# Prologue of an adaLN, linear-attention and MLP block: three query chunks folded in 64 by 64 tiles, modulation rows paired, layer-norm statistics moved

## The chip, the cores and the metric

The kernel runs on one core of one Trainium2 chip. The metric is the device time of one execution in microseconds. The core has five engines that this text names as its profile does: PE (TensorE; PEld is its weight load), DVE (VectorE), ACT (ScalarE), POOL (GpSimd) and SP (SyncE, which here only issues DMAs).

## The reference, cut to what matters

```python
mod = (silu(c) @ w_mod).reshape(1, 6, 1, 640)
sa, ca, ga, sb, cb, gb = mod[:, 0], ..., mod[:, 5]
h = layernorm(x) * (1 + ca) + sa                    # x: 2048 x 640
qkv = h @ wqkv                                      # 32 heads of 20
pq = einsum("bhsd,hdf->bhsf", q, w_phi)             # and pk from k
phi_q = concat([softmax(pq), softmax(-pq)])         # and phi_k from pk
kv = einsum("bhsf,bhsd->bhfd", phi_k, v)
z = phi_k.sum(over s)
o = (phi_q @ kv) / (phi_q . z + 1e-6)
x = x + ga * (o @ wo)
h = layernorm(x) * (1 + cb) + sb
x = x + gb * (relu(h @ w1 + b1) ** 2 @ w2 + b2)     # 640 -> 1728 -> 640
```

## The kernel before

Tokens come in 16 tiles of 128, handled in pairs `j`; the 640 features are five chunks `d` of 128. The feature map `w_phi` is multiplied into the weights of q and k once, at the start ("fold"), so that a projection gives pq and pk at once. Precision is kept by splitting each matrix into a high part in `fp32r` and a low part, the difference; each product is then three matmuls (`three`).

The change touches the prologue, up to the first attention tiles. There the order on all five engines is written out by hand: a `manual_schedule` block (`first`) keeps every engine in program order. So an instruction that waits holds up all that stands behind it on its engine.

The parts of the prologue, in their order:

- `load_raw`, `load_x`, `load_wm`: SP issues the loads: raw k weights, the first token pair `x0`, raw q weights, the modulation weights `wm` of chunks 0 to 4, then `x1` and the v weights. ACT issues two small ones (`bd`, `c`).
- DVE builds `bd_t`, block-diagonal copies of `w_phi`, from `bdc` and a mask that POOL makes.
- Warm-up matmuls (`WARM`, `SHORT`) on PE.
- `fold(nm, d)` (L276): six matmuls of 120 rows by 128 columns, with 120 (once 40) moving columns, into a pair of PSUM tiles. In f32 each matmul is two passes on PE, so a fold shows as 12 records. Its `split` copies both PSUM tiles to the high part on ACT (L283) and takes the low part on DVE (L92).
- `stats` (L556 to L561): mean and variance of a token pair on DVE, then four small POOL instructions; `scale` (L566) normalizes it on ACT. `x0`'s statistics stand behind the split of k's chunk 3.
- `mod_rows2` (L582): the modulation vector of a chunk, c-weighted sums of `wm`, as ten f32 matmuls in four column tiles of 32; `mod_sb` (L590) copies it to SBUF on ACT; `mod_cols2` transposes it on PE (L595) and sums on DVE into `cols_a` (L597).
- `t_in` (L358): PE transposes normalized `x0` into PSUM. `out0(d)` scales and shifts chunk `d` on ACT (`hf`, L369), copies the high part on ACT (`hT`, L370) and takes the low part on DVE (L92).
- `k_step(d)`: chunk `d`'s contribution to k of the first two token tiles, 12 matmuls into four PSUM tiles `pk`.
- Behind the five k steps: ACT casts v's first weight chunk (`v_hi`, L665) and copies k out of PSUM (`to_sb`, L429); DVE and ACT go on to the feature map, and PE to the query projection `do_q(0)` (`pq`).

PSUM tiles of the tag `pj` come in four buffers, two to a fold or projection, taken in turn: `pq`'s first pair is that of the first token tile's `pk`, and the fold of q3 takes the pair of q1. The fold of q0 uses two tiles of another tag, `kvp`. After the prologue PE's order stays fixed, and the other engines' order is set by a planner for a part of the way.

The heart of the prologue's order before:

```python
    for d in range(4):
        fold("k", d)()
    n0 = stats(XB[0], "a0")
    fold("k", 4)()
    fold("q", 0, kvp[1:])()
    fold("q", 1)()
    scale(XB[0], *n0)
    fold("q", 2)()
    split = fold("q", 3)
    mod_rows2(0)
```

Of the kernel before, what the change touches and what calls it, by code (L numbers as in the profile page):

```python
# [12 lines left out]
ALU = mybir.AluOpType  # L13
AX = mybir.AxisListType

P = 128
S = 2048
D = 640
H = 32
DH = 20  # L20
F = 1728
NT = S // P
NC = D // P
NF = 14
FS = [128] * 13 + [64]
GR = [(120 * g, 120) for g in range(5)] + [(600, 40)]
NG = len(GR)
NU = 11
HEAD_AT = [(h % 3 + 3 * (h // 12), h // 3 % 4, h) for h in range(H)]
HEAD_AT.sort()  # L30
HALF = D // 2
# [1 line left out]
V_HEADS = ((0, 19), (19, H - 1))  # L33
EPS = 1e-5
POSTPONED = 4
WARM = 9
SHORT = 7
KEPT = NT - POSTPONED
W2_AT = 48
PLAIN = 2  # L40
# [15 lines left out]
def kernel(  # L56
# [6 lines left out]
    wq1: bass.AP,  # L63
    wv: bass.AP,
    bd: bass.AP,
    c: bass.AP,
    w_ss: bass.AP,
    w_mod: bass.AP,
# [7 lines left out]
    nc = tc.nc  # L76
# [34 lines left out]
    def tok2(tag, name, at=0, pool=None):  # L111

        bufs = 1
        if tag == "w":
            tag = f"w{next(w_at)}"
        elif pool is None:
            bufs = BUFS.get(tag, 1)
        t = (pool or mem).tile([P, 2 * D + (W2_AT if tag == 'late' else 128 if tag in W_LONG else 0)], F32, tag=tag, name=name, bufs=bufs)
        return t[:, at : at + 2 * D].rearrange("p (s d) -> p s d", s=2)

    def row(tag, name):
        return (pc if tag in ("s3", "s4") else mem).tile([P, D], F32, tag=tag, name=name, bufs=BUFS[tag])
# [19 lines left out]
    def tp(name):  # L142
# [4 lines left out]
    kvp = [psK.tile([P, 512], F32, name=f"kvp{b}") for b in range(3)]  # L147
# [6 lines left out]
    ones = const.tile([P, P], F32, name="ones")  # L154
    nc.gpsimd.memset(ones, 1.0)

    bdc = row("s3", "bdc")
# [3 lines left out]
                            pattern=[[-DH, 6]], channel_multiplier=1)  # L161
    nc.gpsimd.affine_select(out=own, in_=own, compare_op=ALU.is_ge, fill=0.0, base=DH - 1,
                            pattern=[[DH, 6]], channel_multiplier=-1)
    ident = const.tile([P, P], F32, name="ident")
    make_identity(nc, ident)
    neg = const.tile([P, P], F32R, name="neg")
    plus = const.tile([P, 1], F32, name="plus")
    nc.gpsimd.memset(plus, 0.0)
# [9 lines left out]

    vt = [pc.tile([P, NU * 64], F32, name=f"vt{i}")[:, : H * (DH + 1)].rearrange("p (h d) -> p h d", d=DH + 1) for i in range(2)]
    rs_q = pc.tile([P, NT, 2 * H], F32, name="rs_q")  # L180
# [20 lines left out]

    nc.scalar.dma_start(bdc[:120, :120], bd)
    nc.scalar.dma_start(c_t, c)
    bd_t = row("s4", "bd_t")
    raw, WM, RV, XB = {}, {}, {}, {}

    def load_raw(nm, w5, w1, ds=range(NC)):
        if 0 in ds:
            raw[nm] = [tok2("w", f"raw_{nm}{i}") for i in range(3)]
            nc.vector.memset(raw[nm][2][:, 1], 0.0)  # L210
        for d in ds:
            nc.sync.dma_start(raw[nm][d // 2][:, d % 2], w5[d * P : (d + 1) * P])
            if d == 0:
                nc.sync.dma_start(raw[nm][2][:40, 1], w1)

    def load_x(j):
        XB[j] = tok2(f"x{j % 2}", f"xb{j}")
# [2 lines left out]
    def load_wm(d):  # L220
        WM[d] = flat(tok2(("k", "k", "q0", "q1", "w")[d], f"wm_{d}"))
        nc.sync.dma_start(WM[d], w_ss[d * P : (d + 1) * P])
# [4 lines left out]
    load_raw("k", wk5, wk1)  # L227
    load_x(0)
    load_raw("q", wq5, wq1, range(4))
    for d in range(2):  # L230
        load_wm(d)
    load_raw("q", wq5, wq1, (4,))
    for d in range(2, NC):
        load_wm(d)
    load_x(1)
    for d in range(NC):
        if d % 2 == 0:
# [28 lines left out]
    def fold(nm, d, p=None):  # L266

        w = wslot(f"w{nm}{d}")
        W[nm, d] = w
        p = p or pj(f"fold{nm}{d}")  # L270
        for g, (o, n) in enumerate(GR):
            if g < 5:
                r = raw[nm][d // 2][:120, d % 2, g * P : (g + 1) * P]
            else:
                r = raw[nm][2][:120, 1, d * P : (d + 1) * P]
            nc.tensor.matmul(  # L276
                p[g // 3][:, (g % 3) * 120 : (g % 3) * 120 + n], r, bd_t[:120, g * 120 : g * 120 + n],
                start=True, stop=True,
            )

        def split():
            for h, (a, b) in enumerate(((0, 360), (360, 640))):
                nc.scalar.activation(w[:, 0, a:b], p[h][:, : b - a], AF.Copy)  # L283
                lo(w[:, 1, a:b], p[h][:, : b - a], w[:, 0, a:b])

        return split
# [261 lines left out]
    def stats(xt, nm):  # L548

        st = small([P, 2, 2, 6], "st", f"st{nm}")  # L550
        mv = small([P, 2, 2], "mv", f"mv{nm}")
        sq = small([P, 2], "sq", f"sq{nm}")
        nb = small([P, 2], "nb", f"nb{nm}")
        for i in range(2):
            for h in range(2):
                nc.vector.bn_stats(st[:, i, h], xt[:, i, h * HALF : (h + 1) * HALF])  # L556
            nc.vector.bn_aggr(mv[:, i], st[:, i])
        nc.gpsimd.tensor_scalar(sq, mv[:, :, 1], EPS, None, op0=ALU.add)
        nc.gpsimd.tensor_tensor(sq, sq, mhalf, op=ALU.pow)
        nc.gpsimd.tensor_tensor(nb, mv[:, :, 0], sq, op=ALU.mult)  # L560
        nc.gpsimd.tensor_scalar(nb, nb, -1.0, None, op0=ALU.mult)  # L561
        return nb, sq

    def scale(xt, nb, sq):
        for i in range(2):
            nc.scalar.activation(xt[:, i], xt[:, i], AF.Identity, bias=nb[:, i : i + 1], scale=sq[:, i : i + 1])  # L566
# [6 lines left out]
    def mod_rows2(*ds):  # L573

        p = tp(f"mrow{ds[0]}")
        for m, d in enumerate(ds):
            MR[d] = p[:, m * P : m * P + P]
            for k in range(NC):
                for s in range(2):
                    c = 2 * (k % 2) + s  # L580
                    a = 256 * k + P * s
                    nc.tensor.matmul(  # L582
                        MR[d][32 * c : 32 * c + 32], cs[:, k : k + 1].to_broadcast([P, 32]), WM[d][:, a : a + P],
                        start=(k < 2 and m == 0), stop=(k >= NC - 2), skip_group_check=True,
                    )

    def mod_sb(*ds):
        for d in ds:
            t = MR[d, "sb"] = row("s1", f"msb{d}")[:, :P]
            nc.scalar.activation(t, MR[d], AF.Identity, bias=plus[:, 0:1])  # L590

    def mod_cols2(*ds):
        at = {d: half(0, 1)[:, P * (d % 2) : P * (d % 2) + P] for d in ds}
        for d in ds:
            nc.tensor.transpose(at[d], MR[d, "sb"], ident)  # L595
        for d, p in at.items():
            nc.vector.tensor_reduce(  # L597
                cols_a.rearrange("p (s d) -> p s d", s=2)[:, :, d],
                p.rearrange("p (h s r) -> p s h r", h=2, s=2)[:, :, :, 0], axis=AX.X, op=ALU.add,
            )  # L600
# [4 lines left out]
    mem.tile([P, 80], F32, tag="gap2", name="gap2", bufs=1)  # L605
    PP = [pj(f"pk{t}") for t in range(0)]

    def k_step(d):
        w = W["k", d]
        for t in range(2):  # L610
            s = slice(t * P, (t + 1) * P)
            for h, (a, b) in enumerate(CUT):
                mm(PP[t][h][:, : b - a], three(HT[0][:, d, 0, s], HT[0][:, d, 1, s], w[:, 0, a:b], w[:, 1, a:b]),
                   first=(d == 0), last=(d == NC - 1))

    def out0(d):
        t_out(cols_a, HT[0], d, "a0", TR[d])

    warm = tp("warm")
    for i in range(WARM):  # L620
        nc.tensor.matmul(warm[:, :P], ones, ones, start=True, stop=True)
    for i in range(SHORT):
        nc.tensor.matmul(warm[:1, :1], ones[:, :1], ones[:, :1], start=True, stop=True)
    for d in range(4):
        fold("k", d)()
    n0 = stats(XB[0], "a0")
    fold("k", 4)()
    fold("q", 0, kvp[1:])()
    fold("q", 1)()
    scale(XB[0], *n0)  # L630
    fold("q", 2)()
    split = fold("q", 3)
    mod_rows2(0)
    mod_sb(0)
    for d in range(NC):
        t_in(XB[0], d, TR[d])
    split()
    mod_cols2(0)
    out0(0)
    mod_rows2(1)  # L640
    mod_sb(1)
    split = fold("q", 4)
    mod_cols2(1)
    split()
    mod_rows2(2)
    mod_sb(2)
    load_x(2)
    PP += [pj(f"pk{t}") for t in range(2)]
    rows_at, cols_at = {1: (3, 4)}, {1: (2,), 2: (3, 4)}
    for d in range(NC):  # L650
        mod_cols2(*cols_at.get(d, ()))
        if d + 1 < NC:
            out0(d + 1)
        if d in rows_at:
            mod_rows2(*rows_at[d])
        k_step(d)
        mod_sb(*rows_at.get(d, ()))
        if d == 1:
            n1 = stats(XB[1], "a1")
        if d == 3:  # L660
            scale(XB[1], *n1)

    def v_hi(d):
        W["v", d] = wslot(f"wv{d}")
# [46 lines left out]
    for t in range(2, NT - 2):  # L711
        j, i = divmod(t, 2)
# [12 lines left out]
        p = proj("v", t, *([(1, 0, lambda: t1(j + 1, 4))] if t == NT - 3 else []))  # L725
# [489 lines left out]
    for j in range(NB):  # L1215
        nxt = j + 1 < NB
        b, c = 2 * j + 5, 2 * j + 6
# [63 lines left out]
        if j == 7:  # L1281
            t2(0, 4)
            p = tp("gbt")[:NC, :P]
# [347 lines left out]
    for j in range(NB):  # L1631
# [5 lines left out]
        for n in range(NP):  # L1637
            down = lambda k: prev and (down_plain if plain(*prev) else down_pair)(*prev, k)
            twice = not plain(j, n)
            m = NP * j + n - NP - 1  # L1640
# [96 lines left out]
    by_hand.__exit__(None, None, None)  # L1737


_INS = ["x", "wk5", "wk1", "wq5", "wq1", "wv", "bd", "c", "w_ss", "w_mod", "wo", "w1", "b1", "w2", "b2"]  # L1740


# [56 lines left out]
```

## Time and profile before

| | us |
|---|---|
| median of 3 runs | 748.23 |
| lowest, highest | 747.89, 750.46 |
| the profiled execution's own time | 746.04 |
| its span, first to last instruction | 744.3 |
| PE busy | 736.7 |
| DVE busy | 599.0 |
| ACT busy | 454.4 |

The granted TensorE clock was 1.00 over the whole span. In a timeline row stand the start, the length, engine, line, operation, the tiles written and read, the count, and in brackets the idle time of the engine ahead of it with what ended it. In the chain of waits stand start, length and the work that the end of the span is traced back to. Matmuls are pipelined and their ends are modelled, so a busy PE says only that something was in it; starts are firmer than ends.

### The profile page before, as it was taken

To read this page: it belongs to the slowest core of one execution; us is meant where nothing else is said; L and a number is where in the kernel's file an instruction comes from. 1 tells how busy PE (TensorE), PEld (TensorE's weight loads), DVE (VectorE), ACT (ScalarE), POOL (GpSimd) and SP (SyncE) were. 2 spreads that over 40 slices of the span, in tenths; PEclk is the share of its full clock that TensorE was granted. 3 is DMA by queue.
4 is the path that set the end of the run, shared out by engine and by line. 5 is a ranking of instruction groups with operands and counts; after the bars stand their busy time and mean duration, and the time that the engine had idled before them with its cause. 6 is when DMAs were issued, how large, how long until landed. Compare 5 with 4: busy or idle time off the path is not lost.

```text
span 744.3 us, 16676 instructions
## 1 busy us (share of the span) xinstructions
PE 736.7 (99%) x6537; PEld 718.8 (97%) x6537; DVE 599.0 (80%) x1089; ACT 454.4 (61%) x1060; POOL 168.1 (23%) x352
## 2 busy tenths in 40 slices
PE   9999999999999999999999999999999999999997
PEld 9999999999999889998999999999999999999997
DVE  6598988978999999999655777877786776777766
ACT  5767666667863365567687667475573747647431
POOL 2001101001000347647303040231321313222110
PEclk9999999999999999999999999999999999999999
DMA  9912341343432354754885567897667768667461
GB/s 325 344 37 107 120 129 56 107 142 108 139 111 72 99 168 167 166 129 107 210 249 169 151 198 260 272 312 210 185 187 200 211 183 241 185 177 215 129 183 36
DMA packets 58801, 126.47 MB, mean 170 GB/s; under 512 B 7438, under 2 KB 16403, under 8 KB 58723
## 3 DMA queue, kind: packets, MB, share of 16 engines
q1 hardware_dynamic: 38636, 79.20, 32.6%
q0 software_dynamic: 17504, 40.90, 21.8%
q10 hardware_dynamic: 2583, 5.30, 1.9%
q8 instruction: 51, 0.84, 0.5%
q14 instruction: 27, 0.22, 0.1%
HBM read 100.74 MB, written 29.89 MB: 176 GB/s over the span
## 4 chain that ended last, share of the span: by engine, by line
PE 83%; DVE 10%; ACT 3%; issue 2%; POOL 1%; DMA 1%; ACTq 0%; DVEq 0%; POOLq 0%
PE up L82 25%; PE acc L82 18%; PE pwo L82 8%; PE pk L82 7%; PE pv L82 5%; PE acc3x L82 5%; PE pq L82 5%; PE te L950 2%; DVE dn L882 1%; DVE sk L444 1%; PE foldk L276 1%; PE numa L82 1%; DVE ek L436 1%; DVE ek L446 1%; DVE scr L880 1%
## 5 line engine op out<-in xcount | busy, mean ns | idle before, releaser
L82 PE MATMUL up<-h,w 128*128 128x256 f32 x1640 | 204.6, 276 | 0.1
L82 PEld LDWEIGHTS up<-h,w 128*128 128x128 f32 x1640 | 196.4, 188 | 0.7 <-DVE h L92 0.5
L1345 ACT ACTIVATE ft<-up,b_t 128x256 f32<-128x256 f32 x104 | 48.9, 471 | 95.7 <-PE up L82 95.3
L82 PE MATMUL acc<-w,ra 128*128 128x384 f32 x452 | 97.4, 335 | 0.0
L1346 DVE TENSOR_TENSOR ft<-ft 128x256 f32<-128x256 f32 x104 | 44.3, 426 | 42.9 <-ACT ft L1345 41.5
L82 PE MATMUL pwo<-wo,ot 128*128 128x384 f32 (+1 forms) x480 | 78.5, 314 | 0.0
L82 PE MATMUL pq<-wq,hT 128*128 128x384 f32 (+1 forms) x480 | 75.6, 312 | 0.0
L82 PEld LDWEIGHTS acc<-w,ra 128*128 128x128 f32 x452 | 72.7, 188 | 0.9 <-DVE ra L92 0.6
L82 PE MATMUL pk<-wk,hT 128*128 128x384 f32 (+1 forms) x480 | 73.1, 309 | 0.1
L82 PEld LDWEIGHTS pwo<-wo,ot 128*128 128x128 f32 x480 | 69.8, 188 | 2.8 <-issue 2.7
L82 PEld LDWEIGHTS pq<-wq,hT 128*128 128x128 f32 x480 | 71.1, 188 | 0.7 <-issue 0.5
L82 PE MATMUL pv<-wv,hT 128*128 128x384 f32 (+1 forms) x480 | 71.7, 307 | 0.0
L82 PEld LDWEIGHTS pk<-wk,hT 128*128 128x128 f32 x480 | 70.4, 188 | 1.0 <-DVE hT L92 0.5
L82 PEld LDWEIGHTS pv<-wv,hT 128*128 128x128 f32 x480 | 70.1, 188 | 0.0
L92 DVE TENSOR_TENSOR ra<-ft,ra 128x384 fp32r<-128x384 f32 (+2 forms) x86 | 36.8, 449 | 32.6 <-ACT ra L1369 18.8
L1455 POOL DMA_DIRECT2D ring_a<-td_a x34 | 18.5, 543 | 117.3 <-PE acc L82 106.3
L1369 ACT ACTIVATE ra<-ft 128x384 fp32r<-128x384 f32 x48 | 25.2, 526 | 28.4 <-DVE ft L1346 22.4
L82 PE MATMUL acc3x<-w,ra 128*128 128x256 f32 x231 | 39.5, 277 | 0.0
L82 PEld LDWEIGHTS acc3x<-w,ra 128*128 128x128 f32 x231 | 37.2, 188 | 0.0
L444 DVE TENSOR_REDUCE sk<-ek 128x64 f32<-128x1280 f32 x16 | 23.7, 1482 | 14.6 <-ACT ek L439 10.1
L1360 DVE TENSOR_TENSOR ft<-ft 128x128 f32<-128x128 f32 x136 | 33.4, 287 | 1.2
L335 POOL TENSOR_SCALAR sma<-sma 128x2 f32<-128x2 f32 x6 | 2.1, 343 | 133.7 <-ACT xb L334 133.7
(258 smaller groups left out, 1448.7 us busy)
## 6 DMA issues: line engine op xcount, KB each, us to landing
ring_c<-td_c POOLq DMA_DIRECT2D x34, 384.0 KB, 3.9
ring_a<-td_a POOLq DMA_DIRECT2D x34, 384.0 KB, 3.4
ring_b<-td_b POOLq DMA_DIRECT2D x34, 256.0 KB, 3.5
esp<-eq SPq DMA_DIRECT2D x12, 640.0 KB
el<-esp SPq DMA_DIRECT2D x12, 640.0 KB
rw<-in_w SPq DMA_DIRECT2D x23, 320.0 KB
wm<-in_w_mod SPq DMA_DIRECT2D x20, 320.0 KB
xb<-in_x SPq DMA_DIRECT2D x8, 640.0 KB
```

Of the source, the lines that this page charges most:

```text
L82: nc.tensor.matmul(o, a, b, start=first and i == 0, stop=last and i == len(terms) - 1, skip_group_check=skip,)
L92: (eng or nc.vector).tensor_tensor(out_lo, full, hi.bitcast(F32), op=ALU.subtract)
L276: nc.tensor.matmul(p[g // 3][:, (g % 3) * 120 : (g % 3) * 120 + n], r, bd_t[:120, g * 120 : g * 120 + n], start=True, stop=True,)
L436: nc.vector.tensor_tensor(heads(e[:, s]), heads(t), over(mx[:, s]), op=ALU.subtract)
L444: nc.vector.tensor_reduce(s, heads(flat(e)), axis=AX.X, op=ALU.add)
L446: nc.vector.tensor_tensor(heads(flat(e)), heads(flat(e)), over(s), op=ALU.mult)
L950: nc.tensor.transpose(p[:124, a : a + P], EU[2 * j + i][:, 2 * g + c, :124], ident)
L1345: nc.scalar.activation(r, p, AF.Relu, bias=b1_t[:, f : f + 1])
L1346: nc.vector.tensor_tensor(r, r, r, op=ALU.mult)
L1360: nc.vector.tensor_tensor(t[:, o], t[:, a], t[:, b], op=op)
L1369: nc.scalar.activation(a[:, 0, :3], t[:, :3], AF.Copy)
L1455: nc.gpsimd.dma_start(RING[j, n, r], TD[n][r].bitcast(F32R))
```

## The change

- Chunks 2, 3 and 4 of q are folded by matmuls of 64 rows by 64 columns with 60 (once 20) moving columns: four at a time, one in each quarter of the array, the two row halves into different PSUM tiles. For that the host lays out the raw q weights of these chunks and a second matrix `bdq` otherwise, DVE builds `bq_t` from it with a mask of POOL's, and two more small DMAs bring `wq4`.
- The order: `x0`'s statistics come behind k's chunk 2 instead of 3; q1's split comes behind `scale`; q2 and q3 are folded back to back with their splits later; q4's fold moves from ahead of the k steps to between the third and the fourth, into other PSUM tiles.
- `mod_rows2` takes chunks 1 and 2 in one call, as it did 3 and 4, and turns the column tiles of every second chunk so that each has equal work. The columns of chunks 3 and 4 come in the middle of the third k step.
- `x1`'s statistics move from behind the second k step to behind chunk 4's `out0`; its scaling from behind the fourth k step to behind the fifth.
- The modulation weights of all five chunks are loaded ahead of q's chunk 4.
- The warm-up has three matmuls of 384 columns in place of nine of 128 and seven of one.

```diff
+Q_FOLDS = [(60 * g, 60) for g in range(5)] + [(300, DH)]
+FOUR = (2, 3, 4)
...
-WARM = 9
-SHORT = 7
+WARM = 3
...
+    own6 = bdc[:, 376:382]
+    own_q = own6[:, :3]
...
+    nc.gpsimd.tensor_tensor(own_q, own_q, own6[:, 3:], op=ALU.add)
...
+    nc.scalar.dma_start(bdc[:, 256:376], bdq)
     bd_t = row("s4", "bd_t")
+    bq_t = row("s4", "bq_t")
...
-    for d in range(2):
+    for d in range(NC):
         load_wm(d)
     load_raw("q", wq5, wq1, (4,))
-    for d in range(2, NC):
-        load_wm(d)
     load_x(1)
...
+        four = nm == "q" and d in FOUR
+        if four:
+            for g, (o, n) in enumerate(Q_FOLDS):
+                r = raw[nm][d // 2][:, d % 2, g * P : (g + 1) * P] if g < 5 else raw[nm][2][:, 1, d * P : (d + 1) * P]
+                for a in (0, 64):
+                    for c in (0, 64):
+                        nc.tensor.matmul(
+                            p[a // 64][c : c + 64, o : o + n], r[a : a + 64, c : c + 64], bq_t[a : a + 64, o : o + n],
+                            start=(g == 0), stop=True, skip_group_check=True,
+                        )
...
-                    c = 2 * (k % 2) + s
+                    c = 2 * ((k + m) % 2) + s
...
-    def k_step(d):
+    def k_step(d, between=None):
         w = W["k", d]
         for t in range(2):
+            if t and between:
+                between()
...
-    for d in range(4):
+        nc.tensor.matmul(warm[:, : 3 * P].rearrange("p (a n) -> p a n", a=3), ones, ones[:, None, :].to_broadcast([P, 3, P]), start=True, stop=True)
+    for d in range(3):
         fold("k", d)()
     n0 = stats(XB[0], "a0")
-    fold("k", 4)()
+    nc.vector.tensor_tensor(
+        bq_t[:, :360].rearrange("p (g i f) -> p g i f", i=3, f=DH),
...
+    )
+    for d in range(3, NC):
+        fold("k", d)()
     fold("q", 0, kvp[1:])()
-    fold("q", 1)()
+    split = fold("q", 1)
     scale(XB[0], *n0)
-    fold("q", 2)()
-    split = fold("q", 3)
+    split()
+    splits = [fold("q", d) for d in range(2, 4)]
     mod_rows2(0)
     mod_sb(0)
     for d in range(NC):
         t_in(XB[0], d, TR[d])
-    split()
+    splits[0]()
     mod_cols2(0)
     out0(0)
-    mod_rows2(1)
-    mod_sb(1)
-    split = fold("q", 4)
+    splits[1]()
+    mod_rows2(1, 2)
+    mod_sb(1, 2)
     mod_cols2(1)
-    split()
-    mod_rows2(2)
-    mod_sb(2)
     load_x(2)
     PP += [pj(f"pk{t}") for t in range(2)]
-    rows_at, cols_at = {1: (3, 4)}, {1: (2,), 2: (3, 4)}
-    for d in range(NC):
-        mod_cols2(*cols_at.get(d, ()))
-        if d + 1 < NC:
-            out0(d + 1)
-        if d in rows_at:
-            mod_rows2(*rows_at[d])
-        k_step(d)
-        mod_sb(*rows_at.get(d, ()))
-        if d == 1:
-            n1 = stats(XB[1], "a1")
-        if d == 3:
-            scale(XB[1], *n1)
+    out0(1)
+    k_step(0)
+    mod_cols2(2)
+    out0(2)
+    k_step(1)
+    mod_rows2(3, 4)
+    mod_sb(3, 4)
+
+    def late_cols():
+        mod_cols2(3, 4)
+        out0(3)
+
+    k_step(2, late_cols)
+    out0(4)
+    n1 = stats(XB[1], "a1")
+    fold("q", 4, (kvp[1], tp("foldq4")))()
+    k_step(3)
+    k_step(4)
+    scale(XB[1], *n1)
```

More of the change, by code (lines that the diff above doesn't have):

```diff
@@ L65 @@
     bd: bass.AP,
+    bdq: bass.AP,
+    wq4: bass.AP,
     c: bass.AP,
@@ L165 @@
     make_identity(nc, ident)
+    own6 = bdc[:, 376:382]
+    own_q = own6[:, :3]
+    o6 = own6.rearrange("p (a i) -> p a i", a=2)
+    nc.gpsimd.memset(own6, 1.0)
+    nc.gpsimd.affine_select(out=o6, in_=o6, compare_op=ALU.is_ge, fill=0.0, base=0,
+                            pattern=[[-64, 2], [-DH, 3]], channel_multiplier=1)
+    nc.gpsimd.affine_select(out=o6, in_=o6, compare_op=ALU.is_ge, fill=0.0, base=DH - 1,
+                            pattern=[[64, 2], [DH, 3]], channel_multiplier=-1)
+    nc.gpsimd.tensor_tensor(own_q, own_q, own6[:, 3:], op=ALU.add)
     neg = const.tile([P, P], F32R, name="neg")
@@ L212, in load_raw @@
             nc.sync.dma_start(raw[nm][d // 2][:, d % 2], w5[d * P : (d + 1) * P])
-            if d == 0:
+            if d == 0 and nm == "k":
                 nc.sync.dma_start(raw[nm][2][:40, 1], w1)
+            elif d == 0:
+                n = FOUR[0] * P
+                nc.sync.dma_start(raw[nm][2][:40, 1, :n], w1[:, :n])
+                for a in range(2):
+                    nc.sync.dma_start(raw[nm][2][64 * a : 64 * a + DH, 1, n:], wq4[DH * a : DH * a + DH, n:])
     def load_x(j):
@@ L270, in fold @@
         p = p or pj(f"fold{nm}{d}")
[L271 to L279, printed above, removed]
+        four = nm == "q" and d in FOUR
[8 more added lines that the diff above has]
+                        )
+        else:
+            for g, (o, n) in enumerate(GR):
+                if g < 5:
+                    r = raw[nm][d // 2][:120, d % 2, g * P : (g + 1) * P]
+                else:
+                    r = raw[nm][2][:120, 1, d * P : (d + 1) * P]
+                nc.tensor.matmul(
+                    p[g // 3][:, (g % 3) * 120 : (g % 3) * 120 + n], r, bd_t[:120, g * 120 : g * 120 + n],
+                    start=True, stop=True,
+                )
+        half_ = HALF if four else 360
         def split():
-            for h, (a, b) in enumerate(((0, 360), (360, 640))):
+            for h, (a, b) in enumerate(((0, half_), (half_, D))):
                 nc.scalar.activation(w[:, 0, a:b], p[h][:, : b - a], AF.Copy)
@@ L620 @@
     for i in range(WARM):
-        nc.tensor.matmul(warm[:, :P], ones, ones, start=True, stop=True)
-    for i in range(SHORT):
-        nc.tensor.matmul(warm[:1, :1], ones[:, :1], ones[:, :1], start=True, stop=True)
-    for d in range(4):
+        nc.tensor.matmul(warm[:, : 3 * P].rearrange("p (a n) -> p a n", a=3), ones, ones[:, None, :].to_broadcast([P, 3, P]), start=True, stop=True)
+    for d in range(3):
         fold("k", d)()
     n0 = stats(XB[0], "a0")
-    fold("k", 4)()
+    nc.vector.tensor_tensor(
+        bq_t[:, :360].rearrange("p (g i f) -> p g i f", i=3, f=DH),
+        bdc[:, 256:376].rearrange("p (g f) -> p g f", f=DH)[:, :, None, :].to_broadcast([P, 6, 3, DH]),
+        own_q[:, None, :, None].to_broadcast([P, 6, 3, DH]), op=ALU.mult
+    )
+    for d in range(3, NC):
+        fold("k", d)()
     fold("q", 0, kvp[1:])()
-    fold("q", 1)()
+    split = fold("q", 1)
     scale(XB[0], *n0)
-    fold("q", 2)()
-    split = fold("q", 3)
+    split()
+    splits = [fold("q", d) for d in range(2, 4)]
     mod_rows2(0)
@@ L1737 @@
     by_hand.__exit__(None, None, None)
-_INS = ["x", "wk5", "wk1", "wq5", "wq1", "wv", "bd", "c", "w_ss", "w_mod", "wo", "w1", "b1", "w2", "b2"]
+_INS = ["x", "wk5", "wk1", "wq5", "wq1", "wv", "bd", "bdq", "wq4", "c", "w_ss", "w_mod", "wo", "w1", "b1", "w2", "b2"]
 def kernel(A_x, A_wqkv, A_w_phi, A_wo, B_x, B_w1, B_b1, B_w2, B_b2, c, w_mod):
@@ L1752 @@
         bd[h % 6, :, h // 6] = A_w_phi[h]
+    bdq = np.zeros((2, 64, 6, DH), A_w_phi.dtype)
+    for h in range(H):
+        a, k = divmod(h, H // 2)
+        bdq[a, DH * (k % 3) : DH * (k % 3 + 1), k // 3] = A_w_phi[h]
     b1 = np.zeros((NF * P,), B_b1.dtype)
@@ L1761, in by_chunk, with by_half @@
         return t.reshape(P, 5, NC, P).transpose(2, 0, 1, 3).reshape(NC * P, D), w.T[600:]
+    def by_half(w):
+        w = w.T.reshape(2, HALF, D)
+        t = np.zeros((2, 64, 5, D), w.dtype)
+        t[:, :60] = w[:, :300].reshape(2, 5, 60, D).transpose(0, 2, 1, 3)
+        return t.reshape(P, 5, NC, P).transpose(2, 0, 1, 3).reshape(NC * P, D), w[:, 300:].reshape(2 * DH, D)
     wq5, wq1 = by_chunk(A_wqkv[:, :D])
+    wq5h, wq4 = by_half(A_wqkv[:, :D])
+    wq5 = np.concatenate([wq5[: FOUR[0] * P], wq5h[FOUR[0] * P :]])
     wk5, wk1 = by_chunk(A_wqkv[:, D : 2 * D])
@@ L1778 @@
         "bd": bd.reshape(120, 120),
+        "bdq": bdq.reshape(P, 120),
+        "wq4": wq4,
         "c": c.reshape(NC, P).T,
```

## The prediction

> **What bounds the kernel now.** I read four views in this order: the page's first part, the chain of waits over the first 60 us, the engines' timelines over the first 75 us, and PE's waits after that. The change lies wholly in the prologue, so the question is what sets each PE step there.
>
> ```profile
> PE 736.7 (99%) x6537; PEld 718.8 (97%) x6537; DVE 599.0 (80%) x1089; ACT 454.4 (61%) x1060; POOL 168.1 (23%) x352
> ```
>
> Chain of waits, start and length in us:
>
> ```profile
> 1.05 3.80 PE warm L621 x18
> ...
> 12.09 1.34 PE kvp L276 x12
> 13.43 4.02 PE foldq L276 x36
> 17.45 0.78 PE mrow L582 x20
> 18.23 1.24 PE kvp L358 x10
> 19.47 0.11 PE kvp L595
> 19.58 0.78 PE mrow L582 x20
> 20.36 1.46 PE foldq L276 x12
> ...
> 22.73 1.93 PE pk L82 x12
> 24.67 0.11 PE kvp L595
> 24.78 1.43 PE mrow L582 x40
> 26.21 1.92 PE pk L82 x12
> 28.14 0.22 PE kvp L595 x2
> 28.35 5.18 PE pk L82 x36
> 33.53 4.31 PE pq L82 x30
> ```
>
> The chain is PE alone from 1.05 us: folds, modulation rows, transposes, five k steps, then at 33.53 the first query projection. PE work taken out here shortens the kernel, but only if nothing on ACT or DVE takes its place. Waits of PE's weight loads from 30 to 260 us are short:
>
> ```profile
> PEld kvp L453 <- issue: 1.3, 2, 0.9
> PEld tail L932 <- DVE ut L905: 1.0, 1, 1.0
> PEld pk L82 <- DVE hT L92: 0.5, 2, 0.4
> ```
>
> So a PE delay at 33.53 has little idle time behind it to be absorbed in, and ACT and DVE work that hangs on it is late by as much. I pass it on in full.
>
> ACT's timeline, the rows that matter:
>
> ```profile
> 15.46 1.73 ACT L566 ACTIVATE xb<-xb,nba,sqa 128x640 f32<-128x640 f32 x2 [0.25 <-POOL nba L561]
> 17.10 0.74 ACT L283 ACTIVATE wq<-foldq 128x360 fp32r<-128x360 f32 x2
> 18.28 0.37 ACT L590 ACTIVATE msb<-mrow,plus 128x128 f32<-128x128 f32 x1 [0.44 <-PE mrow L582]
> 20.04 0.56 ACT L369 ACTIVATE hfa<-kvp,cols_a 128x256 f32<-128x256 f32 x1 [0.74 <-DVE cols_a L597]
> 20.63 0.42 ACT L370 ACTIVATE hT<-hfa 128x256 fp32r<-128x256 f32 x1
> ...
> 30.46 1.74 ACT L566 ACTIVATE xb<-xb,nba,sqa 128x640 f32<-128x640 f32 x2
> 32.10 0.72 ACT L665 ACTIVATE wv<-rawv 128x640 fp32r<-128x640 f32 x1
> 32.73 1.39 ACT L429 ACTIVATE k<-pk 128x384 f32<-128x384 f32 x4
> ```
>
> DVE's:
>
> ```profile
> 4.31 0.85 DVE L244 TENSOR_TENSOR bd_t<-bdc 120x360 f32<-120x360 f32 x2 [2.05 <-POOL mask L190]
> ...
> 9.35 0.98 DVE L92 TENSOR_TENSOR wk<-foldk,wk 128x360 fp32r<-128x360 f32 x2 [0.35 <-ACT wk L283]
> ...
> 11.59 0.87 DVE L556 BATCH_NORM_STATS2 sta<-xb 128x6 f32<-128x320 f32 x2
> ...
> 13.62 0.84 DVE L92 TENSOR_TENSOR wk<-foldk,wk 128x360 fp32r<-128x360 f32 x2
> ...
> 17.58 0.89 DVE L92 TENSOR_TENSOR wq<-foldq,wq 128x360 fp32r<-128x360 f32 x2 [1.53 <-ACT wq L283]
> ...
> 19.85 0.15 DVE L597 TENSOR_REDUCE cols_a<-kvp 128x2 f32<-128x4 f32 x1
> ...
> 26.40 0.88 DVE L556 BATCH_NORM_STATS2 sta<-xb 128x6 f32<-128x320 f32 x2
> ...
> 30.55 0.43 DVE L92 TENSOR_TENSOR hT<-hfa,hT 128x256 fp32r<-128x256 f32 x1 [0.48 <-ACT hT L370]
> ```
>
> The reader should see one thing above all: x1's scaling (ACT, 30.46) starts 4.06 us after x1's statistics begin on DVE (26.40), and behind it on ACT stand the first v weight (32.10) and the copies of k out of PSUM (32.73). The first query projection needs the first of those PSUM tiles; all four "pj" tiles hold k by then. Before, the copy came just in time.
>
> **The change part by part.**
>
> *Tiled folds (q2, q3, q4).* A fold is 12 passes in 1.34 us, 0.112 each (row at 12.09). It becomes 48 passes in four tiles, 12 to a tile. Nearest rows: the kv products in four column tiles, and four row tiles at once:
>
> ```profile
> 60.44 1.41 PE kvp L453 x125
> ```
> ```profile
> L818 PEld LDWEIGHTS z<-kvs,ident x8: 180/182/184, 246.5 to 246.6; 21*128 21x128 f32 x8
> ```
>
> The kv passes (40 moving columns) cost 1.41 over 32 to a tile, 0.044. The modulation rows (128 columns, 12 passes in the fullest tile) cost 1.43/12 = 0.119. For 60 columns that interpolates to 0.061, for 20 I keep 0.044: 10 x 0.061 + 2 x 0.044 = 0.70 us a fold. Eight weight loads of z start within 0.1 us, so row tiles overlap too; no row here has 64 by 64. Ends: 48 x 0.0113 = 0.54 below; above, passes one after the other at half a full pass, 48 x 0.056 = 2.7. I take 0.70, near the kv row. PE work saved: 0.64 for each of q2 and q3, 0.76 for q4.
>
> Switching between tiled and untiled work has a price in the chain: a k step behind modulation rows took 1.93, the three at 28.35 only 5.18/3 = 1.73, so 0.2 at most a switch. The Trainium skill (TensorEngine Tiling (Array Packing), Key Properties) says that changing the tiling mode drains TensorE; the 0.2 agrees, and by that rule the added switch around q4 costs 0.2.
>
> *Modulation sums of two chunks.* The rotation gives each tile 10 passes where one had 12: 1.43 becomes 1.2 (10 x 0.119). Chunks 1 and 2 together: 1.2 for 2 x 0.78. Saved: 0.36 and 0.23. Between nothing and this.
>
> *Statistics of x0 one chunk sooner.* They can start when k2's low half is done (9.35 + 0.98 = 10.33) and x0 is there. Ahead of x0 lie k's 1.74 MB and its own 0.66, plus 0.06 for the new matrix:
>
> ```profile
> 0.00:10.00 10.00, 8.95 (x75) 8.79 (x76) 5.20 (x14) 4.31 (x9) 4.06 (x29) 1.00 0.80 254
> ```
>
> At 254 GB/s, 2.46 MB are there at 9.7, and some tenths go until the wait ends; I take 10.6 (10.3 to 11.0). From statistics to scaling took 15.46 - 11.59 = 3.87, so scaling starts at 14.5 (before 15.46). But q1's split now stands behind the scaling on ACT; before, it came ahead. Its copies start 17.10 - 15.46 = 1.64 later, at 16.1; its low half ends 1.37 later (17.10 to 17.58 + 0.89), 17.5. Fold q3 needs q1's two PSUM tiles. PE is through q1 at about 15.0 (0.3 of that is k3's low half, now behind the statistics and the new matrix, on whose tile q1 waits) and through q2 at 15.7. It waits 1.8 us; q3 ends at 18.2 where before it ended at 17.45: **+0.75**. The saving of two tiled folds is gone.
>
> *To the first k step.* Rows, transposes and columns of chunk 0 as before, so columns end at 19.58 + 0.75 = 20.33. Rows 1 and 2 run to 21.5. ACT meanwhile: row copy 0 (to 19.45), q2's copies (0.74, to 20.1); DVE's q2 low half (to 20.75) precedes the column sum at 20.7; hf and hT of chunk 0 to 21.9 (before 20.04 to 21.05 with the sum at 19.85); q3's copies (0.74) to 22.6; only then row copy 1 (0.37), to 22.9. PE needs it for columns 1: a wait of 1.4. First k step at about 23.05, before 22.73: **+0.3**.
>
> *To the columns of chunks 3 and 4 (call their end C; before 28.35).* After 23.05: k step 1.93, columns 0.11, k step 1.75, rows 1.2, half a k step 0.97, columns 0.22: C = 29.2, **+0.9**. Fold q4 is no longer before C, but half a k step is.
>
> *x1's statistics behind chunk 4.* This is the step that decides. Before, they ran at 26.40, ahead of C. Now they stand on DVE behind chunk 4's low half. Chunk 4's low half ends 30.98 - 28.35 = 2.63 after C; statistics to scaling 4.06 (3.87 by x0); scaling and first v weight, up to the first copy of k, 32.73 - 30.46 = 2.27. First copy at C + 8.8 to 9.0 = 38.1, before 32.73. On PE, from C: 0.87 + 0.7 (q4) + 0.2 + 2 x 1.73 = 5.2, so k is done at 34.4 and PE stands still for about 4 us until the copy frees the tile. **Sum: 38.1 - 32.73 = +5.4**, taken as +5.2 since the copy had a little slack before. Fold q4's saving lies inside this wait and counts for nothing.
>
> *At no cost,* and what covers it:
>
> ```profile
> 4.76 0.21 ACT L257 ACTIVATE ce<-c_t 128x5 f32<-128x5 f32 x1 [1.57 <-DMA c_t<-in_c]
> ```
> ```profile
> 13.80 0.24 POOL L558 TENSOR_SCALAR sqa<-mva 128x2 f32<-128x2 f32 x1 [8.06 <-DVE mva L557]
> ```
>
> The warm-up (18 passes of 128 columns become 6 of 384, again about 3.8 us) ends before bd_t is built (4.31 + 0.85, and its last piece); if the clock came up later for it, some tenths. The build of bq_t on DVE, about 0.5 by bd_t's 360 columns, lies in the k3 delay above. Four GpSimd instructions more: GpSimd idles 8 us ahead of x0's statistics. One DMA issue more on ACT: it waits 1.57 for c. Two small ones more on SP: chunk 2's modulation load behind them is wanted 1.4 us sooner than before, but q4's 0.33 MB (1.3 us at 254 GB/s) no longer stands ahead of it. The load of q4 itself moves behind 2 MB, at most 8 us at that rate; its fold was at 20.36 without a wait and comes after 30 now.
>
> The profiled execution took 746.04 (span 744.3), 2.2 below the runs' median of 748.23. 746.04 + 5.2 = 751.2; on the runs' scale **753.4**.
>
> **The rivals.**
> *PE's work sets the time* (not slower). If k's copies weren't behind the scaling, the PE sums would stand: 2 x 0.64 + 0.36 + 0.23 + 0.76 = 2.6 less, 745.6; with the two earlier waits still there, +0.9 or so, 749.1. For it: the chain is PE alone. Against: ACT's rows keep program order, and the point of decision is C <= 23.8 (32.73 - 8.96), 4.5 us sooner than before, while PE's work alone, without any wait, puts C at 25.8 (13.43 + 1.34 + 1.4 + 2.13 + 1.31 + 2.04 + 2.95 + 1.19). 0.16.
> *The two early waits are hidden, the late one stays.* C = 25.8, first copy at 34.7: +2.0, 750.2. It needs q1's split ahead of the scaling. 0.13.
> *The clock falls in the 4 us wait.* At the start 18 passes took 3.80, where 18 x 0.112 = 2.0 is full speed: 1.8 lost until the clock came up. If the wait sends it back, +7.0, 755.2. No wait of this trace is long enough to show it. The Trainium skill (TensorE: Matmul & The Clock Gate, Why this matters for your kernels) bears on it: one idle window, gaps over about 3 us, halves the clock again. 0.15.
> *Tiles run one after the other.* q2 and q3 then take 5.4 us from 15.0, to 20.4 in place of 18.2: C is 2.2 later, +7.4, 755.6; q4's 2.7 fit in the late wait. 0.04.
>
> **How the numbers follow.** The likeliest (0.52) is the late stall with the clock held: 753.4, its own range 752.0 to 754.6. From 748.5 to 756.5 leaves out the gain of 2.6 (half of the first rival) and about as much again in the tails of the terms bounded above. What 0.5% (3.7 us) can tell from no change: slower holds nearly all of the likeliest, the clock and the serial tiles (0.66); within it lie the first two rivals and the likeliest's lower tail (0.31); faster by 3.7 is more than all PE savings together (0.03).
>
> **What would show it.** PE idle of about 4 us ahead of the first query projection (pq), near 34 to 38; x1's scaling near 36, the first k copy near 38; PE waits of 1 to 2 us ahead of the last tiled fold of the prologue's first part and ahead of the columns of chunk 1; a tiled fold near 0.7. The prediction is wrong if the k copies start before 35, if q3 follows q2 at once, or if a later stage takes up the delay.

## The result, and the profile after

| | median, us | lowest to highest | runs |
|---|---|---|---|
| before | 748.25 | 747.89 to 750.46 | 4 |
| after | 757.40 | 756.33 to 759.96 | 4 |

The changed kernel takes 1.0121 times as long (interval 1.0089 to 1.0153): 9.15 us slower, where 5.2 was forecast. The profiled execution after took 757.19 (span 755.5), close to its median; the one before was 2.2 below its own.

The page after shows little more work:

```profile
PE 741.1 (98%) x6619; PEld 720.5 (95%) x6619; DVE 599.9 (79%) x1090; ACT 454.0 (60%) x1060; POOL 168.6 (22%) x356
```

PE is busy 4.4 us longer, with 82 instructions more of its own. The prologue shows why: its timeline on PE (columns: start, length, then the work, and in brackets the idle time ahead of it):

```profile
14.25 1.53 PE L304 MATMUL foldq<-bd_t,raw_q 120*128 120x120 f32 x12
15.71 0.89 PE L294 MATMUL foldq<-bq_t,raw_q 64*64 64x60 f32 x48
17.98 1.23 PE L294 MATMUL foldq<-bq_t,raw_q 64*64 64x60 f32 x48 [1.38 <-DVE wq L95]
19.14 0.85 PE L612 MATMUL mrow<-wm,cs 128*32 128x128 f32 x20
23.74 0.33 PE L625 MATMUL kvp<-ident,msb 128*128 128x128 f32 x1 [1.17 <-ACT msb L620]
23.82 1.98 PE L85 MATMUL pk<-wk,hT 128*128 128x384 f32 x12
29.80 0.38 PE L625 MATMUL kvp<-ident,msb 128*128 128x128 f32 x2
31.79 3.73 PE L85 MATMUL pk<-wk,hT 128*128 128x384 f32 x24
39.32 7.04 PE L85 MATMUL pq<-wq,hT 128*128 128x384 f32 x30 [3.80 <-ACT k L459]
...
70.30 4.68 PE L85 MATMUL pq<-wq,hT 128*128 128x384 f32 x30
```

The same places before, in PE's timeline:

```profile
13.26 4.19 PE L276 MATMUL foldq<-bd_t,raw_q 120*128 120x120 f32 x36
22.66 2.00 PE L82 MATMUL pk<-wk,hT 128*128 128x384 f32 x12
33.37 4.47 PE L82 MATMUL pq<-wq,hT 128*128 128x384 f32 x30
...
61.77 4.57 PE L82 MATMUL pq<-wq,hT 128*128 128x384 f32 x30
```

Three waits are new: 1.38 ahead of the last tiled fold, 1.17 ahead of the columns of chunk 1, 3.80 ahead of the query projection, all where forecast. But that projection then runs 7.04 where it ran 4.47. What releases it, in ACT's timeline after:

```profile
36.54 1.73 ACT L596 ACTIVATE xb<-xb,nba,sqa 128x640 f32<-128x640 f32 x2 [3.56 <-POOL nba L591]
38.18 0.72 ACT L704 ACTIVATE wv<-rawv 128x640 fp32r<-128x640 f32 x1
38.80 1.39 ACT L459 ACTIVATE k<-pk 128x384 f32<-128x384 f32 x4
```

ACT stands idle for 3.56 us ahead of x1's scaling, with the copies of k behind it; before, they began at 32.73.

Why the projection is slow, in the windows view of after (stretch and length; busy time of PE, PEld, DVE, ACT, POOL with instructions in brackets; granted clock; DMA share; GB/s):

```profile
34.44:37.85 3.41, 1.08 (x8) 0.88 (x7) 1.10 (x4) 1.31 (x2) 1.35 (x4) 1.00 0.34 129
37.85:41.26 3.41, 1.94 (x6) 1.94 (x7) 2.30 (x4) 3.41 (x8) 0.00 (x0) 0.50 0.01 2
41.26:44.67 3.41, 3.41 (x13) 3.41 (x12) 3.41 (x5) 2.88 (x6) 0.00 (x0) 0.50 0.00 0
44.67:48.09 3.42, 3.42 (x30) 3.42 (x29) 3.39 (x6) 2.07 (x5) 0.00 (x0) 1.00 0.00 0
```

From 37.85 the clock is at half for 6.83 us. In the wait it costs nothing; from 39.32 to 44.67 it does: 13 matmuls in 3.41 us where the next stretch has 30.

Starts differ between executions by up to 3 us with the arrival of the first loads and the clock's first rise, so what follows goes by intervals inside one execution: **A** from the start of q1's fold to the first k step, **B** from there to the first query projection, **C** from there to the third one. Each is a difference of two row starts like those above: before, A = 22.66 - 13.26 = 9.40, B = 33.37 - 22.66 = 10.71, C = 61.77 - 33.37 = 28.40; after, A = 9.57, B = 15.50, C = 30.98.

| kernel | q1's fold starts | A | B | C | median (runs) | ratio to before [95%] |
|---|---|---|---|---|---|---|
| before | 13.26 | 9.40 | 10.71 | 28.40 | 748.25 (4) | |
| before, another execution (e9) | 13.86 | 9.41 | 10.70 | 28.40 | 749.21 (1) | |
| after | 14.25 | 9.57 | 15.50 | 30.98 | 757.40 (4) | 1.0121 [1.0089, 1.0153] |
| after, another execution (e10) | 15.39 | 10.94 | 15.50 | 30.97 | 758.80 (1) | |
| e1, scaling late | 13.91 | 10.96 | 11.56 | 28.40 | 748.29 (10) | 1.0011 [0.9999, 1.0024] |
| e2, wait filled | 15.33 | 9.58 | 15.51 | 28.52 | 755.54 (4) | 1.0114 [1.0085, 1.0144] |
| e3, statistics late alone | 13.18 | 9.41 | 14.84 | 30.18 | 754.02 (4) | 1.0091 [1.0068, 1.0114] |
| e4, old warm-up | 14.17 | 10.96 | 15.51 | 31.13 | 758.95 (4) | 1.0150 [1.0126, 1.0173] |
| e5, q1's split first | 15.07 | 8.69 | 11.56 | 28.83 | 747.34 (10) | 0.9992 [0.9981, 1.0003] |
| e6, all waits out | 13.67 | 8.63 | 12.35 | 28.41 | 747.33 (12) | 0.9992 [0.9981, 1.0004] |
| e7, tiles alone | 14.23 | 8.63 | 10.77 | 28.83 | 746.53 (12) | 0.9982 [0.9968, 0.9995] |
| e8, tiles, rotation, scaling late | 16.03 | 8.63 | 10.70 | 28.40 | 747.95 (12) | 1.0001 [0.9988, 1.0014] |
| e11, scaling late alone | 14.01 | 9.40 | 10.72 | 28.40 | 748.94 (12) | 1.0010 [0.9997, 1.0022] |

Each ratio is to runs of before made beside that kernel's. Their medians were 747.19 for e1 to e4, 748.26 for e5 to e7 and 748.44 for e8 and e11, so medians of different sets aren't to be subtracted.

### The profile page after: what moved, and what is told of

It reads as the page before. It is cut to its first block, busy times and chain, and to the rows that moved or that the text cites. A ratio compares the mean times of both kernels' runs of the same rounds, so it can differ in the third digit from the quotient of the medians.

```text
span 755.5 us, 16841 instructions
## 1 busy us (share of the span) xinstructions
PE 741.1 (98%) x6619; PEld 720.5 (95%) x6619; DVE 599.9 (79%) x1090; ACT 454.0 (60%) x1060; POOL 168.6 (22%) x356
## 4 chain that ended last, share of the span: by engine, by line
PE 85%; DVE 6%; ACT 4%; issue 1%; DMA 1%; POOL 1%; ACTq 0%; SPq 0%; DVEq 0%
PE up L85 25%; PE acc L85 18%; PE pv L85 8%; PE pk L85 8%; PE pwo L85 8%; PE pq L85 7%; PE acc3x L85 5%; PE te L989 2%; PE kvp L483 1%; DVE dn L921 1%; DMA xb<-in_x 1%; PE numa L85 1%; DVE scr L919 1%; PE ta L388 1%; PE numb L85 1%
## 5 line engine op out<-in xcount | busy, mean ns | idle before, releaser
L85 PE MATMUL pq<-wq,hT 128*128 128x384 f32 (+1 forms) x480 | 79.9, 323 | 3.8 <-ACT k L459 3.8
L85 PEld LDWEIGHTS pq<-wq,hT 128*128 128x128 f32 x480 | 75.3, 197 | 4.7 <-ACT k L459 4.0
```

The source lines that it names most:

```text
L85: nc.tensor.matmul(o, a, b, start=first and i == 0, stop=last and i == len(terms) - 1, skip_group_check=skip,)
```

## The experiments

My theory after the result: x1's scaling ahead of k's copies makes the wait of 3.8 us (B), and the wait makes the clock fall (C). The rival for the rest was that the changed warm-up, the early waits or the new order cost by themselves.

**e1, scaling late** (from after):

```diff
     k_step(4)
-    scale(XB[1], *n1)
...
         to_sb(PP[t], PK[t])
+    scale(XB[1], *n1)
```

> The changed kernel with one move: x1's scaling stands behind the copies of k out of PSUM on ACT, not ahead of them. Theory A (the late copies hold up PE, and the wait sends the clock down): the 3.8 us wait ahead of the first query projection shrinks to under 0.5, the first query projection starts near 35.5 us in place of 39.3 and takes 4.5 in place of 7.0; the time falls by 6 to 8 us against the changed kernel, to 749 to 751.5. Theory B (the loss is made after the prologue, by the planner's other order): the prologue gains but the total stays above 754. Theory C (something else holds PE there, such as the fold of chunk 4): the wait stays.

PE and ACT timelines of e1:

```profile
36.43 4.47 PE L85 MATMUL pq<-wq,hT 128*128 128x384 f32 x30
```
```profile
35.42 1.63 ACT L459 ACTIVATE k<-pk 128x384 f32<-128x384 f32 x4 [0.74 <-PE pk L85]
37.78 1.73 ACT L596 ACTIVATE xb<-xb,nba,sqa 128x640 f32<-128x640 f32 x2 [0.73 <-POOL nba L591]
```

The copies now wait for PE, not PE for them. B falls from 15.50 to 11.56 and C is back at 28.40, and the ratio goes from 1.0121 to 1.0011: moving this one line removes nearly the whole loss (a part of that lies behind the third projection, see below). Its A is 1.4 longer than in the first trace of after, though the code there is the same. The windows of e1 show it:

```profile
15.22:18.63 3.41, 2.00 (x95) 1.72 (x95) 1.47 (x4) 2.10 (x4) 0.00 (x0) 1.00 1.02 412
18.63:22.05 3.42, 3.42 (x45) 2.91 (x37) 0.87 (x2) 1.02 (x3) 0.00 (x0) 0.50 1.01 407
```

The wait of 1.38 ahead of the last tiled fold lies in the first stretch; in the next the clock is at half.

**e2, wait filled** (from after). Six matmuls whose result nothing uses run in the wait; they change no order on ACT:

```diff
     k_step(4)
+    for i in range(6):
+        nc.tensor.matmul(kvp[0][:, : 3 * P]..., ones, ones[:, None, :].to_broadcast([P, 3, P]), start=True, stop=True)
     scale(XB[1], *n1)
```

> The changed kernel with six f32 matmuls of ones by 384 columns (results unused) behind the fifth k step, about 3.8 us of PE work in place of the idle wait. Nothing else moves: the copies of k still come near 38.8. Theory A, the part on the clock: the granted clock stays at 1.00 through 35 to 50 us, the first query projection still starts near 39.3 but takes 4.5 us, not 7.0; the total falls by 2.6 (and by up to 1.7 more if the second drop near 160 us does not come), to 753 to 755. Theory D (the slow projection has another cause than the idle wait): it takes 7.0 again and the total is 757.

PE's timeline and the windows of e2:

```profile
36.45 4.03 PE L701 MATMUL kvp<-ones 128*128 128x384 f32 x12
40.42 4.58 PE L85 MATMUL pq<-wq,hT 128*128 128x384 f32 x30
```
```profile
38.04:41.45 3.41, 3.41 (x14) 2.17 (x13) 1.42 (x2) 3.41 (x8) 0.00 (x0) 1.00 0.01 2
```

The wait is as long as ever (B = 15.51), the clock holds, and C is 28.52: the slow projection is the clock's doing, and it costs 30.98 - 28.52 = 2.5. The ratio fell only to 1.0114, well inside the interval of after's, and the median lies just above the range that was expected. Against e4, which ran beside the same runs of before but has another warm-up too, it is 3.4 us less; A and C, 1.4 and 2.6 shorter in the traces, would make 4.0. So the price of the clock is shown by the intervals, and in the times only as compatible with them.

**e3, statistics late alone** (from before). Nothing of the tiles, the loads or the other order:

```diff
         if d + 1 < NC:
             out0(d + 1)
+        if d == 3:
+            n1 = stats(XB[1], "a1")
...
-        if d == 1:
-            n1 = stats(XB[1], "a1")
-        if d == 3:
+        if d == 4:
             scale(XB[1], *n1)
```

> The kernel before with one part of the change alone: x1's statistics behind the low half of chunk 4 on DVE, and x1's scaling behind the fifth k step on ACT. Theory A: the first copy of k comes 4 to 4.5 us later than before, PE waits about 4 us ahead of the first query projection, and the clock drops behind the wait: 4.3 + 2.6 = 6.9 slower than before, 754 to 756. If the wait falls so that the clock holds: 752 to 753. Theory B or C: within 1.5 us of before.

PE's timeline and the windows of e3:

```profile
37.43 6.21 PE L82 MATMUL pq<-wq,hT 128*128 128x384 f32 x30 [3.96 <-ACT k L429]
```
```profile
34.62:38.04 3.42, 0.61 (x3) 0.61 (x4) 1.00 (x2) 3.39 (x7) 0.00 (x0) 1.00 0.09 33
38.04:41.45 3.41, 3.41 (x13) 3.41 (x12) 3.38 (x5) 3.27 (x6) 0.00 (x0) 0.50 0.03 7
```

This one edit gives 1.0091, some 6.8 us: B is 4.1 longer, C 1.8, together 5.9; the rest lies elsewhere (see the planner's order under e11). The clock stayed down for one stretch here and for two after the whole change; in both, the stretch after which it rose again had PE busy throughout.

**e4, old warm-up** (from after: `WARM = 9`, `SHORT = 7` and the loops of before).

> The changed kernel with the warm-up of before (nine matmuls of 128 columns, seven of one). If the three wide matmuls are why the clock came up only during the first fold, near 7.3 us in place of 4.3: full clock near 4.3, first folds 0.8 us earlier, and the total 0.8 lower, 756.5. If the moment is set by something that differs from run to run: no difference in the mean, and the folds may be slow here too.

The ratio is 1.0150 [1.0126, 1.0173], not better than after's. The wait of 3.81 and the two falls of the clock are there as in e10. The new warm-up isn't what costs.

**e5, q1's split first** (from e1):

```diff
-    split = fold("q", 1)
+    fold("q", 1)()
     scale(XB[0], *n0)
-    split()
```

> The changed kernel with x1's scaling late (as in e1_scale_late) and q1's split ahead of x0's scaling on ACT, as it stood before. Theory A for the first wait (fold q3 waits for q1's PSUM tiles, whose split stands behind the scaling): the wait of 1.4 us ahead of the second tiled fold goes (under 0.3 left), and with it the clock drop that e1_scale_late showed at 18.6 to 22.0 us; q projection starts 1 to 2.5 us sooner than in e1_scale_late (36.4), the total falls by about as much, to 746 to 747.5. If the wait has another cause (DVE's backlog behind the statistics): no change.

PE's timeline of e5 has both tiled folds in one group:

```profile
16.54 2.16 PE L294 MATMUL foldq<-bq_t,raw_q 64*64 64x60 f32 x96
```

The wait of 1.38 is gone and A falls from 10.96 to 8.69; 1.4 of these 2.3 is the clock that now holds. A and B together are 20.25, where before has 20.11: q4's fold now stands in B. The median is 747.34, ratio 0.9992: no loss, no gain that can be told.

**e6, all waits out** (from e5):

```diff
-    splits[1]()
     mod_rows2(1, 2)
     mod_sb(1, 2)
+    splits[1]()
```

The build of `bq_t` also moves from behind x0's statistics to right behind that of `bd_t`.

> As e5_q1_split_first, and besides: the row copies of chunks 1 and 2 ahead of q3's split on ACT, and bq_t built behind bd_t on DVE, not ahead of k3's low half. Theory A: the wait ahead of the columns of chunk 1 (1.2) and the one ahead of fold q1 (0.5) go; PE then keeps its savings of about 2.5 us, the first query projection starts near 32 (33.4 before) and the total is 1 to 2.5 below before, 744.7 to 746.2. Theory B (the planner's order behind the prologue eats it): the projection starts sooner but the total is that of before or more.

PE's timeline of e6 ahead of the first k step:

```profile
20.31 1.44 PE L617 MATMUL mrow<-wm,cs 128*32 128x128 f32 x38 [0.56 <-issue]
22.22 0.33 PE L630 MATMUL kvp<-ident,msb 128*128 128x128 f32 x1 [0.47 <-ACT msb L625]
22.30 2.17 PE L85 MATMUL pk<-wk,hT 128*128 128x384 f32 x12
```

The waits weren't all out. A stays at 8.63: a wait of 0.56 ahead of the paired rows and one of 0.47 ahead of the columns remain. B grows to 12.35: the second k step starts 2.54 behind the first, where e5 has 1.87, and waits for chunk 1's `hT`, whose column sum on DVE (23.59) now stands behind q3's low half (22.78). A and B together are 0.87 longer than before's, not shorter. Same time as e5; the gain that was expected didn't come.

**e7, tiles alone** (before, with `bq_t` built behind `bd_t` and q2, q3, q4 folded in tiles; order, loads of `wm`, warm-up, scaling as before).

> The kernel before with one part of the change alone: chunks 2, 3 and 4 of q folded in 64 by 64 tiles, in before's order of work, loads and warm-up. Three folds take 0.7 to 0.9 in place of 1.34 to 1.46. If PE alone sets the prologue's time: 1.5 to 2 us faster than before, 745.3. If PSUM tiles and ACT set it once PE is quicker (the folds then wait for the splits, 1.0 to 1.3 us a chunk on ACT and DVE): within 0.5 us of before. Slower by 1 to 2 if the mixed work lets the clock drop.

PE's timeline of e7:

```profile
15.68 2.27 PE L302 MATMUL foldq<-bq_t,raw_q 64*64 64x60 f32 x96
17.88 0.85 PE L620 MATMUL mrow<-wm,cs 128*32 128x128 f32 x20
```

Two tiled folds take 17.88 - 15.68 = 2.20, 1.10 each, where an untiled one took 1.34 and 0.7 to 0.9 was expected. All three save 0.77 in A. The ratio of 0.9982 is the best of all kernels run, about 1.3 us less than before, its interval just clear of 1; as the best of ten versions it may owe some of that to chance.

**e8, tiles, rotation, scaling late** (from e7: `c = 2 * ((k + m) % 2) + s`, and x1's scaling behind k's copies).

> The version that the runs so far point to: before's order, the three tiled folds (as in e7_tiles_alone), the modulation rows with equal work in the column tiles, and x1's scaling behind the copies of k on ACT. PE's work ahead of the first query projection is 0.2 less than in e7_tiles_alone, and ACT's copies no longer stand behind the scaling: projection at 32.5 to 33.5, total 0 to 1 below e7_tiles_alone, 745.5 to 746.5, 1.5 to 2.5 below before. If the planner's order behind the prologue decides: anywhere within 2 us of before.

A and B are in sum the shortest of all, 0.07 below e7's, yet the median is 747.95, ratio 1.0001, above the range that was expected. In the profiled execution the clock first reached full speed at 10.6 us, so q1's fold started at 16.03; that is the run's, since e7 has the same code up to there.

**e11, scaling late alone** (from before).

> The kernel before with x1's scaling alone moved behind the copies of k on ACT. If the copies were just in time before, PE gains nothing: within 0.5 us of before. If they held PE up: up to 0.5 us faster.

```profile
33.12 1.62 ACT L429 ACTIVATE k<-pk 128x384 f32<-128x384 f32 x4 [1.23 <-PE pk L82]
```

In ACT's timeline the copies now wait 1.23 for PE; A, B and C stay as before, and so does the time (1.0010). The scaling had just fitted ahead of the copies.

This run and e8 have something else in common with the changed kernel: the order that the planner gives ACT and DVE behind the prologue. Going by operation and tile names, the traces hold only two such orders. e1, e5, e6 and e7 have the one of before; after, e2, e3, e4, e8 and e11 have another. ACT's timelines show the first difference, before and then after: a pass over `eq` comes ahead of a copy of k, no longer behind it.

```profile
56.17 0.39 ACT L429 ACTIVATE k<-pk 128x256 f32<-128x256 f32 x1 [0.77 <-PE pk L82]
57.90 0.72 ACT L439 ACTIVATE eq<-eq 128x640 f32<-128x640 f32 x1
```
```profile
63.82 0.73 ACT L469 ACTIVATE eq<-eq 128x640 f32<-128x640 f32 x1
64.70 0.39 ACT L459 ACTIVATE k<-pk 128x256 f32<-128x256 f32 x1
```

From the start of the third projection to the end, the five traces with before's order and no fall of the clock ahead of the last 2 us took 681.8 to 682.9 (before, e1, e5, e6, e7); the five with the other order took 683.3 to 684.6 (e2, e3, e4, e8, e10). That is some 1.6 in the mean, from one trace of each. In the times only e11 has this order with A, B and C as before: 0.7 slower, in an interval from 0.2 faster to 1.6 slower. So the second order seems to cost about 1 us, which no experiment isolates.

**e9 and e10**, the two kernels unchanged, once more:

> The kernel before, unchanged, for a second trace. Half of its runs showed a mean granted clock of 0.997 and 748 to 750 us, the other half 1.000 and 746 to 747. If this run is of the first half, its trace should show one stretch of 3.4 us at half clock somewhere, and where; if of the second, none.

> The changed kernel, unchanged, for a second trace. Theory A: the wait of about 3.8 us ahead of the first query projection is there again and the clock falls in it again, since the wait takes most of a 3.4 us stretch whatever its start; the moment at which the clock first comes up, and a second drop near the kv products, may differ.

PE's timeline and the windows of e9 around 150 us:

```profile
152.89 6.16 PE L82 MATMUL pq<-wq,hT 128*128 128x384 f32 x30
```
```profile
149.40:152.81 3.41, 2.04 (x66) 1.72 (x66) 1.89 (x4) 1.50 (x5) 0.90 (x2) 1.00 0.01 2
152.81:156.22 3.41, 3.41 (x13) 3.41 (x12) 1.14 (x2) 2.85 (x5) 0.00 (x0) 0.50 0.93 295
```

A projection that took 4.62 in the first trace of before takes 6.16 here: before has falls of the clock too, behind the kv products. The first trace of after has one at the same place (160.73), so that one isn't the change's. The windows of e10:

```profile
16.45:19.86 3.41, 2.00 (x81) 1.72 (x84) 1.73 (x5) 2.34 (x4) 0.00 (x0) 1.00 0.98 326
19.86:23.27 3.41, 3.41 (x62) 2.90 (x52) 0.40 (x1) 1.02 (x3) 0.00 (x0) 0.50 1.01 404
36.93:40.34 3.41, 1.10 (x9) 0.90 (x7) 1.12 (x4) 1.29 (x2) 1.35 (x4) 1.00 0.06 21
40.34:43.75 3.41, 1.92 (x6) 1.92 (x7) 2.28 (x3) 3.41 (x8) 0.00 (x0) 0.50 0.01 5
```

The same kernel falls at q3's wait in this execution (19.86) and didn't in the first; both fall at the long wait.

## Why the prediction was right or wrong

The direction, the place and the main mechanism were right; the size was 4 us short, outside the range. The step that failed is **the choice of the likeliest case, "the late stall with the clock held"**: the clock fell. That was the rival "the clock falls in the 4 us wait", and its price, too, was too small: with the 2.58 that was measured it gives 748.23 + 5.2 + 2.58 = 756.0, and the last 1.4 of the 757.40 lie in the smaller terms below.

- *x1's statistics behind chunk 4.* Scaling "near 36", first copy "near 38", PE idle about 4 us: measured 36.54, 38.80, 3.80. The sum makes B 4.9 longer (5.2 less the 0.3 that lies ahead of the first k step); measured 4.79. e1 and e3 show the cause from both sides.
- *The clock.* Priced at 1.8 by the slow warm-up; measured 2.58 in C after the change, 2.57 in e10, removed by e2. The 1.8 was the loss of one slow stretch, which e3 also has (1.78). Here the clock stayed down for two stretches, and the wait still filled part of the first; in e3, where the wait was over 0.6 us before the fall, it stayed down for one. That this is the reason fits all traces but wasn't tested. The 4 us wait itself has no row before, but the price of a second stretch could have been put into the range.
- *The wait of q3.* "1.8 us", measured 1.38; e5 shows that q1's split behind the scaling makes it. Missed: in e1, e4 and e10 the clock falls behind it as well, which lengthens A by 1.4. I asked what the clock does in the 4 us wait alone.
- *The columns of chunk 1.* "1.4", measured 1.17. *The first k step* "+0.3": A is 0.17 longer.
- *What lies ahead of q1's fold.* Taken at 0.3, "some tenths" more if the clock came up later. In the four traces with before's order there q1's fold started at 13.18 to 14.01, in the seven with after's at 13.67 to 15.39: about 1.0 more in the mean. But e7 and e8, which do the folds in before's order too and add only the build of `bq_t` and the loads for the tiles, started at 14.23 and 16.03. Part of the difference is the wait for k3's low half (0.33 to 0.58 in five of them), as forecast; part is waits for the first loads, which some executions have and others don't. This isn't settled.
- *The sum.* Intervals: 4.8 (B) + 2.6 (C) + 0.2 to 1.5 (A) = 7.6 to 8.9. About 1.0 ahead of them and about 1 behind them (the planner's other order, which the prediction doesn't have) would make 9.6 to 10.9. The medians differ by 9.15, so the two terms of 1 aren't both shown in full. "Passed on in full" held in that nothing was made up behind: from the third projection to the end, after took 685.2 and 684.3, before 682.5 and 685.1, with a fall of the clock in the first and the last of these.
- *Tiled folds.* "0.70": 31.79 - 30.97 = 0.82 for q4 between k steps, 1.10 between untiled folds and rows (e7). The saving of all three together is 0.77 (e7), not 2.04. The rival "PE's work sets the time" had 2.6 less; the nearest to it is e8, whose A and B are 0.78 shorter than before's and whose time is that of before.
- *The switch around q4,* put at 0.2: in e1 the two k steps behind the tiled fold took 36.43 - 32.86 = 3.57 against 2 x 1.75 before ((33.37 - 28.11) / 3), so at most 0.1 of it shows there. The Trainium skill (TensorEngine Tiling (Array Packing), Key Properties) has a change of tiling mode drain TensorE; no run here shows the drain by itself.

That e5 and e6 are no faster than before needs no other cause: their way to the first query projection (A and B) isn't shorter. e8's is, by 0.78, but it has the planner's other order behind. That the one cancels the other isn't shown: no run of e8's prologue had before's order.

## What to carry to other kernels

Where an engine keeps program order, ask of each moved instruction what stands behind it: here a scaling that waits for late statistics held up a copy that PE needed, and one line put behind that copy gave nearly all of it back. A PE wait is to be priced with the clock: its own length, and here up to 2.6 us of slow work behind it. Much shorter waits can count too: the clock fell behind the wait of 1.38 in three of the five traces that have it. Look also at what a planner makes of the moved line further on. Compare intervals inside one execution, from row to row, before explaining differences of the ends.

## What the runs showed of the hardware

- The clock fell at fixed points of a grid: in each trace every fall lies a whole number of 3.413 us after the first rise to full speed (after: 7.13 + 9 x 3.413 = 37.85; e1: 4.98 + 4 x 3.413 = 18.63; e9: 6.03 + 43 x 3.413 = 152.8). The first rise came between 3.90 (e3) and 10.6 us (e8) over the traces, with either warm-up, so the same wait meets the grid differently in each execution. Ahead of the first rise the clock column reads 1.00 as well, although the 18 passes of before's warm-up took 3.80, 0.21 each, and a fold's 12 took 1.34, 0.11 each, later: the 1.00 over the whole span of before leaves its first 4 us out.
- Ahead of the kernel's last 2 us, each fall followed a stretch of the grid in which PE was busy for 0.61 to 2.04 of 3.41 us; a single wait of 1.38 lay in some of them (e1, e4, e10). Not every such stretch was followed by a fall: in e2 the one from 15.77, with the same wait, had 2.03, in e3 the one from 154.09 had 1.91, and the clock held. The Trainium skill (TensorE: Matmul & The Clock Gate, Why this matters for your kernels) has the clock halved by one idle window, gaps of over about 3 us: the long wait agrees, the falls behind q3's wait and behind the kv products don't, and the measurement decides.
- The clock column showed 0.50 for one stretch (3.41 us) when PE was busy throughout it (e1, e3, e9) and for two when it wasn't (after, e10). What exactly the clock's rule counts isn't shown.
